# Another DMA queue for the weights, earlier weight conversion and another split of the first transpose, in a fused gated linear attention and MLP kernel

## The chip, the cores and the metric

The kernel runs on one core of a Trainium2 chip. The metric is the device time of one execution in microseconds; the time before is the median of five runs.

## The reference, cut to what matters

```python
B, H, S, D = (4, 8, 768, 48)               # attention, float32
f = 1.0 / (1.0 + np.exp(-f_logit))
for t in range(S):
    state = f[:, :, t, :, None] * state + np.einsum('bhd,bhe->bhde', k[:, :, t], v[:, :, t])
    y[:, :, t] = np.einsum('bhd,bhde->bhe', q[:, :, t], state)
x = y.transpose(0, 2, 1, 3).reshape(B * S, H * D)    # 3072 tokens x 384
h = x @ w_in                                # 384 x 2048
g = h * (1.0 / (1.0 + np.exp(-1.702 * h)))
out = g @ w_out                             # 2048 x 384
```

The inputs q, k, v, f_logit are random in float32. The MLP weights come in float64 and are made float32 on the chip.

## The kernel before, in words

The 3072 tokens are cut into 12 units of 256 tokens (4 batches of 3). A unit has an attention part and an MLP part. `attention(n)` gives a list of parts for unit n, and `merge(n, fill, ...)` plays them in order and puts MLP matmuls of earlier units, taken from the list `fill`, between them. So TensorE (PE) does the attention of unit n and the MLP of unit n-1 and before in one stream. Units 0 to 3 are emitted under an order written out by hand for all engines (`fill_order`); from there on only PE's order is by hand. Each engine takes its queue in order.

**Attention of a unit.** Raw gates f, queries q and keys k are loaded by SP (`load_raw`; L260 for the first three units, L267 after) and transposed: in units 0 to 2 by PE and ACT (L344, L349), from unit 3 on by DVE (L332). The gates of unit 3 go through a sigmoid on ACT (L337, which needs a table load before and after it among the MLP's activations). POOL multiplies gates in pairs (`begin_gates`, tile tot, L383). Then come six levels in pairs of tokens, quads and so on: ACT sets the keys of a level aside (tile Kc, L448, queries Qc L454), PE makes scores (sc, L392), DVE multiplies queries and keys by the gates in place (tile X: L473 in units 0 to 2, L477 after) and puts the scores into A (L421, L441). At the end of a unit PE computes y from A and v (L488) and the change of the state (L576), DVE updates the state st (L591, L594, L595), and PE adds the state's share to y (L616). L616 of a unit is emitted after the first promotion L477 or L473 of the next unit.

**The bridge.** y lies in PSUM. It is copied to SBUF as yT (L627), eight copies of 48 rows x 256 elements, one for each of two directions, two groups of 128 tokens and two halves of the heads. In unit 0 four of these are on ACT and four on DVE, in turn. Then `to_x` moves yT into xT, the MLP's input, with six DMAs (L649, L654): from SP's queue, but from ACT's in unit 0. PE then makes h from xT and w_in (L785), ACT the activation g (L789), PE the output o from g and w_out (L811), and ACT or DVE gather sums (L848, L850).

**The weights.** They come in 16 pairs of 128-row blocks, in order: two pairs of w_in, two of w_out, and so on. `fetch_weights` loads the 64-bit words of a pair into one of three buffers (tile bits); the first pair goes over ACT's queue, the others over SP's. A pair of w_in takes two DMAs, one of w_out one. `convert` does one step of a pair at a time: ACT's L217, then on DVE L219 and L220 (shift and mask, integer), L221 (reads bits, and so frees the buffer) and L222 (writes w_in or w_out). When a pair is through, the next fetch is asked for. How many steps go into which unit is said in the calls of `merge`: the argument `pieces` times two is the number of steps, and `by` tells in which share of the unit they should be over. Before, unit 1 takes 24 steps, unit 2 takes 20 and unit 3 takes 14.

From unit 3 on an output unit is done with seven products instead of eight (L762), for which DVE makes sums of w_out blocks (tiles T, L679) after the weights are there.

Of the kernel before, what the change touches and what calls it, by code (L numbers as in the profile page):

```python
# [16 lines left out]
def view(t, offset, dims):  # L17

    a = t[:]
    return bass.AP(a.tensor, a.offset + offset, [list(a.ap[0])] + [list(d) for d in dims])  # L20
# [3 lines left out]
def kernel(  # L24
# [33 lines left out]
    nc = tc.nc  # L58
    B, H, S, D = q.shape
    DM = H * D  # L60
# [4 lines left out]
    U = 256  # L65
# [3 lines left out]
    NP = H // 2  # L69
    HS = 64  # L70
    LEV = [1 << i for i in range(C.bit_length() - 1)]
    NL = len(LEV)
    NK = DM // P
# [60 lines left out]
    at = [wp.tile([P, n], I32, tag="bits", name=f"at{j}", bufs=PAIRS_AHEAD) for j, n in enumerate((1, NL * 64))]  # L134
# [16 lines left out]
    def query(n, f):  # L151

        return ((2, 3), (4, 5) if n < N_FILL else (0, 5))[n % 2][f]
# [16 lines left out]
    for r in range(NGR):  # L170
        ffs = range(r * FG, (r + 1) * FG)
        for ff in ffs[::2]:
            f = slice(ff * P, (ff + 2) * P)
# [9 lines left out]
    fetched, todo = {}, []  # L183
    state = {"fetch": 0, "begin": 0, "done": 0}

    def fetch_weights(engine=nc.sync):
        n = state["fetch"]
        if n >= len(pairs):
            return
        state["fetch"] += 1  # L190
        dst, parts = pairs[n]
        if moe_w_in.dtype == F32:
            for part, src in parts:
                nc.sync.dma_start(out=part(dst), in_=src)
            return
        bits = wp.tile([P, 2 * DM * 2], I32, tag="bits", name=f"bits_{n}", bufs=PAIRS_AHEAD)
        by_dst = bits.rearrange("p (c f) -> p c f", c=dst.shape[1])
        for part, src in parts:
            engine.dma_start(out=part(by_dst), in_=src.bitcast(I32))
        fetched[n] = by_dst.rearrange("p c (f two) -> p c f two", two=2)  # L200
# [25 lines left out]
    def convert():  # L226

        if state["begin"] < len(pairs) and len(todo) <= NOP // 2:
            begin_pair(state["begin"])
            state["begin"] += 1  # L230
        if todo and todo[0]:
            todo.pop(0)()
        if todo and todo[0] is None:
            todo.pop(0)
            state["done"] += 2
            fetch_weights()
# [63 lines left out]
    def rows(h):  # L300
        return slice(h * HS, h * HS + D)
# [4 lines left out]
    def attention(n):  # L306
# [10 lines left out]
        t = {"tms": [F]}  # L317
        parts = []

        def part(kind):  # L320
            return lambda fn: parts.append((kind, fn))
# [85 lines left out]
        def columns(h, g):  # L407

            return rows(h ^ g)
# [188 lines left out]
        @part("W")  # L598
        def _():

            py = t["py"]
            for cs in ((1, 0), (2, 3)):
                for a in range(NP):
                    for c in cs:
                        g, f = CHUNK[c]
                        w = HS
                        if t["before"][c] is None:
                            if not n:  # L610
                                continue
                            w = 1
                        for h in range(2):
                            state = t["before"][c][rows(h), a] if w > 1 else t["ahead"][rows(h), NC - 1, a]
                            x = a * HALF + g * HS
                            nc.tensor.matmul(  # L616
                                py[columns(h, g), g, a, f, :w], lhsT=state, rhs=X[rows(h), query(n, f), x:x + w],
                                start=False, stop=True, skip_group_check=True,
                            )
            yT = att.tile([P, NP, NG, G], F32, tag="kn", name=f"yT_{n}", bufs=1)  # L620
            xT = xTs[n] = mlp.tile([P, NK, width(n)], F32, tag="xT", name=f"xT_{n}", bufs=3)
            for f in (1, 0):
                for g in range(NG):
                    for h in range(2):
                        at, step = (g * HS, 1) if f else (U - 1 - g * HS, -1)
                        copy = nc.vector.tensor_copy if n == 0 and h else nc.scalar.copy
                        copy(view(yT[rows(h)], at, [[U, NP], [step, HS]]), py[columns(h, g), g, :, f, :])  # L627
            to_x(lambda h: (yT[rows(h), :NK], lambda r, d: yT[r:r + d, NK]), xT[:, :, :U], NG)
            if n == NALL - 1:

                pl = ps.tile([P, NP], F32, tag="mm", name="y_last", bufs=4)
                for a in range(NP):
                    for h in range(2):
                        nc.tensor.matmul(
                            pl[rows(h), a:a + 1], lhsT=last["st"][rows(h), NC - 1, a], rhs=q_end[rows(h), a:a + 1],
                            start=True, stop=True,
                        )
                yl = att.tile([P, NP], F32, tag="q_last", name="yT_last", bufs=1)
                for h in range(2):
                    nc.scalar.copy(yl[rows(h)], pl[rows(h)])  # L640
                yl = yl.rearrange("p (a g t) -> p a g t", g=1, t=1)
                to_x(lambda h: (yl[rows(h), :NK], lambda r, d: yl[r:r + d, NK]), xT[:, :, U:], 1)

        def to_x(y, x, ng):

            queue = nc.sync if n else nc.scalar
            for h in range(2):
                most, rest = y(h)
                queue.dma_start(out=x[h * D:(h + 1) * D].rearrange("p c (g t) -> p c g t", g=ng), in_=most)  # L649
                at = 0  # L650
                while at < D:
                    c, p = (h * D + at) // DR, (h * D + at) % DR
                    w = min(D - at, DR - p)
                    queue.dma_start(  # L654
                        out=x[D2 + p:D2 + p + w, c].rearrange("p (g t) -> p g t", g=ng), in_=rest(h * HS + at, w)
                    )
                    at += w
# [114 lines left out]
    def width(n):  # L772

        return U + (n == NALL - 1)
# [80 lines left out]
    def mlp_blocks(*blocks):  # L855

        hs, os = zip(*(mlp_block(n, r) for n, r in blocks))
        return sum(hs, []) + sum(os, [])
# [3 lines left out]
    LAG = 18 * DM  # L862
# [45 lines left out]
    def merge(n, fill, columns, share, pieces=0, hold=0, by=1.0, chores=(), deal=()):  # L908

        parts = parts_of(n)
        total = sum(share(kind) for kind, _ in parts)
        converting = {"W": 3, "T": 3, "B": 1} if n < N_FILL - 1 else {"W": 3, "V": 4, "S": 3, "T": 1, "B": 1}
        total_ops = sum(converting.get(kind, 0) for kind, _ in parts)
        held = sum(share(kind) for kind, _ in parts[:hold])
        at = at_ops = done = ops = 0
        for kind, fn in parts:
            ready = state["done"]
            fn()  # L920
            for chore in chores[:2]:
                chore()
            chores = chores[2:]
            at += share(kind)
            at_ops += converting.get(kind, 0)
            most = pieces * NOP // 2
            n_ops = min(int(most * at_ops / (by * total_ops)), most) - ops
            if deal:
                n_ops, deal = deal[0], deal[1:]
            ops += n_ops  # L930
            first, n_columns = done, max(0, columns * (at - held) / (total - held) - done)

            def some(end):
                nonlocal done
                while fill and done < end and fill[0][2] <= ready:
                    w, emit, _ = fill.pop(0)
                    emit()
                    done += w
            for i in range(n_ops):
                some(first + n_columns * i / n_ops)  # L940
                convert()
            some(first + n_columns)
# [8 lines left out]
    UNIT = NFF * NK * U + U // P * NFF * DM  # L951

    load_raw(0, 0)
    load_raw(0, 2)
    load_raw(0, 1, (nc.scalar,))
    fetch_weights(nc.scalar)
    begin_f, *begin = units[0][0]
    begin_f()
# [5 lines left out]
    load_raw(1, 1)  # L964
    load_raw(1, 2)
    fetch_weights()
    fetch_weights()
    fill = []
# [1 line left out]
    fill += mlp_blocks((0, 0)) + mlp_blocks((0, 1))  # L970
    merge(1, fill, UNIT // 2 - LAG // 2 - 3 * DM, steady, 12, hold=2)
    fill += mlp_blocks((1, 0), (1, 1)) + mlp_blocks((0, 2), (1, 2))
    merge(2, fill, UNIT + 3 * DM, steady, 10)
    fill += mlp_blocks((2, 0), (2, 1)) + mlp_blocks((2, 2), (0, 3)) + mlp_blocks((1, 3), (2, 3))
    merge(3, fill, 3 * UNIT // 2 - LAG // 2, steady, 7, by=0.7)
    fill_order.close()
    for n in range(3, NALL):
        fill += mlp_unit(n)
# [36 lines left out]
```

## Time and profile before

| | |
|---|---|
| median of five runs | 630.69 us (627.81 to 631.24) |
| the profiled execution | 629.54 us, its span 627.8 us |
| PE busy | 605.2 us (96%) |
| DVE busy | 385.9 us (61%) |
| ACT busy | 260.5 us (41%) |
| POOL busy | 39.9 us (6%) |
| granted TensorE clock, mean | 0.984 |
| DMA | 58.21 MB, nearly all on the queue of SP |

Busy time is the time in which an engine has an instruction running; a wait of PE is a gap. "PE h L785" is PE's instruction from line 785 that writes tile h. Tiles are named without their number. An arrow points from what is read to what is written (`out<-in`), or from a waiting instruction to what released it. All times in the stage tables are us from the start of the span.

### The profile page before, as it was taken

To read this page: it belongs to the slowest core of one execution; us is meant where nothing else is said; L and a number is where in the kernel's file an instruction comes from. 1 tells how busy PE (TensorE), PEld (TensorE's weight loads), DVE (VectorE), ACT (ScalarE), POOL (GpSimd) and SP (SyncE) were. 2 spreads that over 40 slices of the span, in tenths; PEclk is the share of its full clock that TensorE was granted. 3 is DMA by queue.
4 is the path that set the end of the run, shared out by engine and by line. 5 is a ranking of instruction groups with operands and counts; after the bars stand their busy time and mean duration, and the time that the engine had idled before them with its cause. 6 is when DMAs were issued, how large, how long until landed. Compare 5 with 4: busy or idle time off the path is not lost.

```text
span 627.8 us, 17094 instructions
## 1 busy us (share of the span) xinstructions
PE 605.2 (96%) x7314; PEld 519.2 (83%) x7314; DVE 385.9 (61%) x632; ACT 260.5 (41%) x544; POOL 39.9 (6%) x91
## 2 busy tenths in 40 slices
PE   7969999889999999999999999999999999999997
PEld 5647776757678688989989989989989889889896
DVE  1879976475876755677566577656658645521441
ACT  3536542533344534543544454354354353233220
POOL 3010110020001001001001001001001001000000
PEclk9968999889999999999999999999999999999999
DMA  6656766642034434444452342542161121001000
GB/s 173 181 154 151 176 148 171 153 114 76 2 92 99 123 102 103 105 97 106 122 135 60 76 108 73 142 122 68 45 160 33 44 59 27 27 1 27 26 1 25
DMA packets 83309, 58.21 MB, mean 93 GB/s; under 512 B 33634, under 2 KB 75266, under 8 KB 83234
## 3 DMA queue, kind: packets, MB, share of 16 engines
q1 hardware_dynamic: 82192, 55.55, 35.1%
q10 hardware_dynamic: 1041, 1.57, 1.0%
q8 instruction: 57, 0.93, 0.6%
q14 instruction: 19, 0.15, 0.1%
HBM read 43.98 MB, written 8.39 MB: 83 GB/s over the span
## 4 chain that ended last, share of the span: by engine, by line
PE 87%; DVE 7%; ACT 3%; DMA 1%; issue 1%; SPq 1%; ACTq 0%; DVEq 0%
PE h L785 38%; PE o_X L762 8%; PE o_Y L762 8%; PE o L811 8%; PE o_Z L762 7%; PE sc L392 6%; PE o_W L762 4%; PE t L344 2%; PE y L616 2%; PE sc L576 2%; PE y L488 1%; ACT yT L627 1%; DVE X L473 1%; DVE a L221 1%; PE idle L108 1%
## 5 line engine op out<-in xcount | busy, mean ns | idle before, releaser
L785 PE MATMUL h<-xT,w_in 128*128 128x256 f32 (+1 forms) x1152 | 259.5, 383 | 2.4 <-ACT g L789 1.9
L785 PEld LDWEIGHTS h<-xT,w_in 128*128 128x128 f32 x1152 | 218.0, 191 | 34.9 <-ACT g L789 2.1
L789 ACT ACTIVATE g<-h 128x256 f32<-128x256 f32 (+1 forms) x192 | 72.2, 384 | 157.8 <-PE h L785 157.6
L477 DVE TENSOR_TENSOR X<-X,tot 128x1024 f32<-128x1024 f32 x45 | 55.1, 1223 | 62.7 <-PE sc L392 49.4
L448 ACT COPY Kc<-X 128x512 f32<-128x512 f32 x72 | 48.0, 666 | 81.4 <-DVE X L477 51.4
L811 PE MATMUL o<-w_out,g 128*128 128x384 f32 x192 | 67.5, 501 | 3.0 <-DVE w_out L222 3.0
L811 PEld LDWEIGHTS o<-w_out,g 128*128 128x128 f32 x192 | 36.3, 194 | 25.9 <-DVE w_out L222 3.6
L762 PE MATMUL o_X<-w_out,g 128*128 128x192 f32 x288 | 52.6, 331 | 0.0
L762 PE MATMUL o_Y<-T,S 128*128 128x192 f32 x288 | 51.9, 329 | 0.0
L441 DVE COPY_PREDICATED A<-masks,sc 128x256 f32<-128x256 uint32 (+1 forms) x108 | 50.9, 535 | 0.1
L762 PEld LDWEIGHTS o_Y<-T,S 128*128 128x128 f32 x288 | 46.9, 190 | 1.5 <-issue 0.7
L762 PEld LDWEIGHTS o_X<-w_out,g 128*128 128x128 f32 x288 | 46.7, 190 | 1.0
L383 POOL TENSOR_TENSOR tot<-F 128x512 f32<-128x512 f32 x12 | 12.5, 1040 | 478.1 <-DVE st L594 428.7
L332 DVE STREAM_TRANSPOSE X<-raw 128x512 f32<-128x512 f32 x36 | 37.9, 1101 | 2.9 <-PE y L616 2.8
L392 PEld LDWEIGHTS sc<-X,Kc 48*64 48x64 f32 x1440 | 26.4, 138 | 14.8 <-ACT Kc L448 8.5
L392 PE MATMUL sc<-X,Kc 48*64 48x64 f32 x1440 | 31.1, 224 | 7.5 <-ACT Kc L448 6.3
L700 DVE TENSOR_TENSOR g<-g,g 128x512 f32<-128x512 f32 x18 | 12.5, 692 | 40.4 <-ACT g L789 40.4
L627 ACT COPY yT<-y 48x256 f32<-48x256 f32 x92 | 33.8, 367 | 8.5 <-PE y L616 6.0
L473 DVE TENSOR_TENSOR X<-X,tot 128x512 f32<-128x512 f32 x30 | 20.4, 690 | 11.2 <-PE sc L392 10.3
L762 PE MATMUL o_W<-T,g 128*128 128x192 f32 x144 | 24.9, 326 | 0.0
L762 PE MATMUL o_Z<-T,g 128*128 128x192 f32 x144 | 24.9, 326 | 0.0
L762 PE MATMUL o_Z<-w_out,g 128*128 128x192 f32 x144 | 24.9, 326 | 0.0
(92 smaller groups left out, 629.2 us busy)
## 6 DMA issues: line engine op xcount, KB each, us to landing
bits<-in_moe_w_out_dram SPq DMA_DIRECT2D x8, 768.0 KB, 5.3
raw<-in_f_logit_dram SPq DMA_DIRECT2D x48, 96.0 KB, 2.3
raw<-in_k_dram SPq DMA_DIRECT2D x48, 96.0 KB, 2.3
raw<-in_q_dram SPq DMA_DIRECT2D x44, 96.0 KB, 2.4
bits<-in_moe_w_in_dram SPq DMA_DIRECT2D x7, 576.0 KB, 5.9
k_tok<-z SPq DMA_DIRECT2D x56, 64.0 KB, 1.7
kt<-k_tok SPq DMA_DIRECT2D x14, 256.0 KB, 2.9
out_dram<-osb SPq DMA_DIRECT2D x18, 192.0 KB, 1.8
```

The source lines that it names most:

```text
L332: nc.vector.transpose(view(out, at, [[HALF, NP], [step, R4], [R4 * step, 32]]), by_half[:, j, f].rearrange("p a (j d) -> p (a j) d", j=R4) ...
L344: nc.tensor.matmul(pt[h * HS:(h + 1) * HS, jj, :], lhsT=by_pair[j][:, h, x:x + HS], rhs=ident, start=True, stop=True)
L392: nc.tensor.matmul(t["sc"][g * HS:(g + 1) * HS, h, a, s, :], lhsT=t["Kc", l][rows(h), x:x + HS], rhs=rhs(h, a, g), start=True, stop=True,)
L441: nc.vector.copy_predicated(out=view(A, at, dims), mask=mask.bitcast(U32), data=got)
L448: nc.scalar.copy(c.rearrange("p (n two m) -> p n two m", two=2, m=m), view(X, KF * SLOT, [[2 * m, SLOT // (2 * m)], [(KR - KF) * SLOT + m, ...
L473: nc.vector.tensor_tensor(x, x, y, ALU.mult)
L477: nc.vector.tensor_tensor(x, x, y, ALU.mult)
L627: copy(view(yT[rows(h)], at, [[U, NP], [step, HS]]), py[columns(h, g), g, :, f, :])
L762: nc.tensor.matmul(t[bank], lhsT=lhs(f), rhs=rhs(f), start=(new and f == 0), stop=(f == HF - 1), skip_group_check=True,)
L785: nc.tensor.matmul(ph, lhsT=w_in[:, c, ff * P:(ff + 1) * P], rhs=xTs[n][:, c, :], start=(c == 0), stop=(c == NK - 1))
L789: nc.scalar.activation(g[ff // FG][:, ff % FG, :], ph, AF.Gelu_apprx_sigmoid)
L811: nc.tensor.matmul(t["po"], lhsT=g[ff // FG][:, ff % FG, tt * P:(tt + 1) * P], rhs=w_out[:, ff, :], start=(ff == ffs[0]), stop=(ff == ffs[ ...
```

## The change

Three things change. `fetch_weights` issues its DMAs from GpSimd's (POOL's) queue instead of SP's; only the first pair stays on ACT's queue. The steps of conversion are dealt out otherwise: unit 2 gets 34 steps (17 x 2), due in 0.9 of the unit, and unit 3 gets none. In unit 0 each of the eight yT copies is cut by pairs of heads: ACT copies the first three pairs (48 rows x 192) and DVE the fourth (48 rows x 64); and the six xT DMAs of unit 0 are issued by SP, as those of all other units are.

```diff
-    def fetch_weights(engine=nc.sync):
+    def fetch_weights(engine=nc.gpsimd):
...
                         at, step = (g * HS, 1) if f else (U - 1 - g * HS, -1)
-                        copy = nc.vector.tensor_copy if n == 0 and h else nc.scalar.copy
-                        copy(view(yT[rows(h)], at, [[U, NP], [step, HS]]), py[columns(h, g), g, :, f, :])
+                        most = NK if n == 0 else NP
+                        nc.scalar.copy(
+                            view(yT[rows(h)], at, [[U, most], [step, HS]]), py[columns(h, g), g, :most, f, :]
+                        )
+                        if n == 0:
+                            nc.vector.tensor_copy(
+                                view(yT[rows(h)], NK * U + at, [[step, HS]]), py[columns(h, g), g, NK, f, :]
+                            )
...
-            queue = nc.sync if n else nc.scalar
             for h in range(2):
                 most, rest = y(h)
-                queue.dma_start(out=x[h * D:(h + 1) * D].rearrange("p c (g t) -> p c g t", g=ng), in_=most)
+                nc.sync.dma_start(out=x[h * D:(h + 1) * D].rearrange("p c (g t) -> p c g t", g=ng), in_=most)
...
-                    queue.dma_start(
+                    nc.sync.dma_start(
...
-    merge(2, fill, UNIT + 3 * DM, steady, 10)
+    merge(2, fill, UNIT + 3 * DM, steady, 17, by=0.9)
...
-    merge(3, fill, 3 * UNIT // 2 - LAG // 2, steady, 7, by=0.7)
+    merge(3, fill, 3 * UNIT // 2 - LAG // 2, steady)
```

## The prediction

> **What bounds the kernel now.** I read the page's first two parts, then busy time by stage, then who waited for whom, then the order of time on ACT and DVE at two places. Columns of the stage rows: start and end, length, busy time (instructions) of PE, its weight loads, DVE, ACT, POOL, then TensorE's granted clock, DMA share and GB/s.
>
> ```profile
> PE 605.2 (96%) x7314; PEld 519.2 (83%) x7314; DVE 385.9 (61%) x632; ACT 260.5 (41%) x544; POOL 39.9 (6%) x91
> ```
> ```profile
> 40.00:60.00 20.00, 15.47 (x185) 12.00 (x185) 17.32 (x30) 10.62 (x20) 0.40 (x2) 0.73 0.58 143
> 60.00:80.00 20.00, 19.26 (x373) 14.52 (x370) 19.11 (x32) 12.04 (x27) 3.09 (x5) 1.00 0.75 171
> 80.00:100.00 20.00, 19.83 (x168) 14.77 (x167) 14.73 (x26) 7.46 (x16) 1.65 (x2) 1.00 0.61 141
> 100.00:120.00 20.00, 18.14 (x129) 12.56 (x128) 12.91 (x20) 9.19 (x14) 0.00 (x0) 0.98 0.68 178
> 120.00:140.00 20.00, 16.87 (x293) 12.02 (x292) 10.51 (x17) 5.71 (x12) 4.19 (x6) 0.85 0.57 138
> ...
> 160.00:180.00 20.00, 20.00 (x139) 14.97 (x139) 17.64 (x24) 5.51 (x12) 0.00 (x0) 1.00 0.13 33
> ```
>
> From 146 us on PE hardly rests (from 300 to 628 us it is busy for 324 of 328). What the change is worth is therefore decided before 146 us, in three places: 37 to 56, where PE waits; 56 to 79, where DVE is full (19.11 of 20) and PE follows it; 116 to 146, where PE waits again. The matmul order of both kernels is the same, row for row.
>
> ```profile
> PE sc L392 <- ACT Kc L448: 6.3, 4, 3.7
> PE o L811 <- DVE w_out L222: 3.0, 1, 3.0
> ...
> PE h L785 <- ACT g L789: 1.9, 1, 1.9
> ...
> PE h L785 <- DMA xT<-yT: 0.5, 1, 0.5
> ```
>
> Those are the waits at 41.6 (3.7 us), 129.1 (3.0), 116.7 (1.9) and 145.5 us. The first, in order of time on ACT, and the third place, on DVE:
>
> ```profile
> 37.47 0.37 ACT L627 COPY yT<-y 48x256 f32<-48x256 f32 x1 [1.37 <-PE y L616]
> 38.33 0.37 ACT L627 COPY yT<-y 48x256 f32<-48x256 f32 x1 [0.49 <-DVE yT L627]
> ...
> 40.44 0.60 ACTq L649 DMA_DIRECT2D xT<-yT  x1
> ...
> 43.34 1.24 ACTq L654 DMA_DIRECT2D xT<-yT  x2
> 44.62 0.67 ACT L448 COPY Kc<-X 128x512 f32<-128x512 f32 x1 [4.21 <-DVE a L221]
> ```
> ```profile
> 126.43 0.35 DVE L595 TENSOR_TENSOR st<-st,sc 128x192 f32<-128x192 f32 x1 [6.28 <-PE sc L576]
> ...
> 129.04 1.72 DVE L221 SCALAR_TENSOR_TENSOR a<-bits,a 128x768 f32<-128x768 uint32 x1
> 130.80 1.25 DVE L222 TENSOR_TENSOR w_out<-a,s 128x768 f32<-128x768 f32 x1
> ...
> 132.64 2.01 DVE L332 STREAM_TRANSPOSE X<-raw 128x512 f32<-128x512 f32 x2
> 136.17 1.23 DVE L477 TENSOR_TENSOR X<-X,F 128x1024 f32<-128x1024 f32 x1 [1.52 <-ACT Qc L454]
> ```
>
> The reader is to see that Kc sits behind six issues on ACT's own queue, and that two engines take yT in strict turns; then that after the last w_out wait (132.1) the same DVE queue still has k's transposes and L477 before y's matmuls, which start at 137.46.
>
> [...]clock 0.50 from 37.3 to 50.9, from 119.2 to 122.6 and from 132.9 to 136.2 us[...].[...] L221, 0.96 us elsewhere, takes 1.72 beside POOL's tot at 128.9.
>
> **Part 1, the first yT and xT.** Now four rounds of ACT 0.37 and DVE 0.42 with 0.03 us between: 0.855 each, 3.42 in all. After: eight rounds of 48x192 on ACT and 48x64 on DVE, and in the built order every one still waits for the one before it on the other engine. ACT: 0.315 (48x256 takes 0.37, 128x192 0.31). DVE: 0.225, an estimate from 0.355 at 192 and 0.42 at 256 elements and 0.19 for a 64-element row. With 0.06 between, 0.60 a round, 4.8 in all: DVE is free **1.38 us later**, at 42.27. What ACT gains: its six issues (40.44 to 44.58) are gone, so Kc starts 0.73 after L473, at 43.0 instead of 44.62, and PE at 43.7 instead of 45.34. But DVE sets the rest of this unit. Its three waits there go: L473 at 45.39 for Kc (0.82 beyond the start-to-start step), at 46.54 (0.54) and 52.70 (0.76) for scores. 2.12 minus 1.38: **0.74 earlier** from 52.7 on, and so through 79 us. On SP the six xT issues, 3.6 us from 41.4, stand ahead of the loads of q and k for unit 2; these are needed at 58 and 72 us, so they cost nothing. xT lands by about 48 to 49; its matmuls can't start before 48.
>
> **Part 2, the queue of the weights.** 22 issues leave SP and stand on POOL between the groups of tot. Each waits for the L221 that frees its buffer, and tot waits behind it: tot of unit 2 (76.6 us) stands behind pair 9, freed at 71.5; tot of unit 3 (128.9) behind pair 15, freed at 105. Nothing waits. Data: pair 7 is freed at 62.6 and needed by ACT at 71 us; it landed 6.3 us after its issue[...]. In unit 2 each pair has 9 us or more.[...] Below: nothing. Above: two of them held for a length each, 1.1 us, for each of some five pairs on the path, 5.6 us. I take **1.0**.
>
> **Part 3, conversions into unit 2.** From L473 at 76.7 to F's transposes at 111.2 DVE now has 13 conversion rows; after, 26. Four rows are 3.06 us start to start, so 10 us more. Its idle time there is 9.3 (1.30, 2.09, 1.71, 1.33, 2.49, 0.36), of which 1.2 stays, before the last scores. So F's transposes start at 111.2 - 0.74 + 10 - 8.1 = 112.4; laid out row by row I get 112.65, ending 114.55. ACT: sigmoid 1.06, then a table load 1.28, but no L217 (0.89) between them any more: g at 116.95 instead of 118.12, matmuls at 117.4, **1.16 earlier** (this holds the 0.74). The idle time is then 1.45 instead of 1.87; I keep the half clock. L595 starts at 125.27.
>
> Behind it w_out no longer keeps PE: the 3.0 go, and **y's matmuls take the wait over**. Between the last st and k's transposes DVE has L220, L221, L222 of pair 15 and a sum, beside tot: 1.3 + 1.25 + 1.15 + 0.46 = 4.2 instead of 3.5; after the transposes two T rows (1.74) fill the 1.52 that ACT needs. L477 comes 0.7 later against L595. PE is out of work at L595 + 5.9 and gets y at L595 + 11.7: 5.8 us idle, so y and the scores after it run at half clock (32 score matmuls: 1.13 instead of 0.69 us at 37.6). y takes 1.8 instead of 1.1, which delays yT and xT by 0.7; scores and 18 o's then make PE itself 0.8 later than xT. Sum at 146 us: -1.16 + 0.7 + 0.7 + 0.8 = +1.04. The relief of DVE after 146 (7 conversion groups, T) buys nothing: PE is full there.
>
> **Sum.** +1.04 + 1.0 = +2.0 against the profiled execution, 629.54 (span 627.8): 631.6. The median shown, 630.69, is 1.15 above it: **632.7**, 0.3% slower, and 0.3% (1.9 us) is about what a measurement of this kernel can tell from no change.
>
> **Rivals.**
> 1. Not slower: the shorter wait for g (1.45) keeps full clock. For it: 0.81 us at 54 and 1.63 at 14.5 did not lower the clock; against: 1.87 did. Then the 1.9 us lost in 18 matmuls (5.84 instead of 3.9) return until DVE binds, its row before L595 ending at 124.0: L595 2.4 earlier, the sum -0.2, and 629.3, or 630.5 by the median. If y too escapes, 1.5 less, 629.0.[...] Chance 0.26.
> 2. [...]its queue in units 1 and 2 is nearly full, so every hold counts: +5.6 instead of 1.0, some 637. For it: L473 2.47 instead of 1.29 beside tot[...]. 0.22.
> 3. Weights come late: if POOL's fetch takes 9 us instead of 6, pair 7 is 1 to 2 us late where DVE is full: 634 to 635. 0.10.
> 4. yT isn't shared at all but taken in turns: that is in my forecast.
>
> **Numbers.** The likeliest case has 0.42, its own range 631 to 634.5, half on each side of 632.6. Range 628.8 to 637. Faster: half of rival 1, 0.12. Same: 0.14 of it and 0.20 of the likeliest, 0.34. Slower: 0.22, 0.22 and 0.10, 0.54.
>
> **What would show it.** yT ends near 42.3 and Kc starts near 43; the wait on w_out at L811 is gone; a wait of PE on L477 of 4 us or more ahead of y; F's transposes end near 114.5; half clock after that wait. I am wrong if h of unit 2 starts before 145 us, if the sixteen yT copies overlap, or if L219 and L220 stay at 0.56 while the time still rises.

## The result and the profile after

| | before | after |
|---|---|---|
| median | 629.65 us (626.88 to 632.42, 79 runs) | 630.84 us (629.2 to 633.98, 44 runs) |
| ratio, 95% interval | | 1.0025 (1.0015 to 1.0034) |
| profiled execution, its span | 629.54, 627.8 us | 631.68, 629.9 us |
| POOL busy | 39.9 us | 54.5 us |

So the change makes the kernel 0.25% slower (0.15% to 0.34%), about the 0.3% that the prediction took as the least that can be told from no change. First the page's busy time and the stage table of the kernel after, with the columns explained in the prediction:

```profile
PE 603.9 (96%) x7314; PEld 519.5 (82%) x7314; DVE 386.5 (61%) x636; ACT 261.3 (41%) x548; POOL 54.5 (9%) x113
```
```profile
40.00:60.00 20.00, 14.64 (x178) 11.64 (x178) 17.44 (x34) 11.73 (x24) 4.77 (x10) 0.83 0.75 156
60.00:80.00 20.00, 19.22 (x378) 14.36 (x375) 19.03 (x32) 11.84 (x26) 5.78 (x8) 1.00 0.61 163
80.00:100.00 20.00, 19.45 (x167) 14.49 (x166) 18.47 (x31) 9.28 (x19) 6.04 (x10) 1.00 0.80 197
100.00:120.00 20.00, 18.00 (x128) 12.11 (x127) 18.84 (x28) 8.43 (x12) 1.46 (x2) 1.00 0.87 201
120.00:140.00 20.00, 13.70 (x226) 10.54 (x230) 18.19 (x26) 6.26 (x13) 4.18 (x6) 0.91 0.42 97
```

DVE is now nearly as full from 80 to 140 us (18.5, 18.8 and 18.2 of 20) as it was before from 60 to 80 alone (19.11). At 80 to 100 the DMA share rose from 0.61 to 0.80. From 120 to 140 PE lost another 3.2 us (16.87 to 13.70). The waits of PE from 30 to 150 us in the kernel after (total us, times, longest):

```profile
PE y L616 <- DVE X L477: 5.6, 1, 5.6
PE sc L392 <- DVE A L421: 4.5, 1, 4.5
PE h L790 <- ACT g L794: 2.7, 1, 2.7
...
PE h L790 <- DMA xT<-yT: 0.4, 1, 0.4
```

The wait on w_out is gone and y waits 5.6 us for L477 in its place. Two waits are new in kind: the first scores of unit 1 wait for A (L421), not Kc, and h waits for xT at 88.6 us. In order of time, DVE in the first unit, then ACT at F, then DVE behind the last state rows, all of the kernel after:

```profile
43.44 0.22 DVE L631 COPY yT<-y 48x64 f32<-48x64 f32 x1 [0.38 <-ACT yT L627]
43.69 1.29 DVE L473 TENSOR_TENSOR X<-X,F 128x512 f32<-128x512 f32 x2
44.90 0.68 DVE L421 TENSOR_TENSOR A<-sc,masks 128x512 f32<-128x512 f32 x1
```
```profile
116.64 1.28 ACT L337 ACT_TABLE_LOAD   x1 [1.68 <-DVE F L332]
117.93 1.06 ACT L337 ACTIVATE F<-F 128x1024 f32<-128x1024 f32 x1
119.00 1.28 ACT L794 ACT_TABLE_LOAD   x1
120.30 0.38 ACT L794 ACTIVATE g<-h 128x256 f32<-128x256 f32 x1
```
```profile
126.92 0.35 DVE L595 TENSOR_TENSOR st<-st,sc 128x192 f32<-128x192 f32 x1 [1.50 <-PE sc L576]
...
129.53 1.32 DVE L220 TENSOR_SCALAR a<-s 128x768 int32<-128x768 int32 x1
130.89 1.25 DVE L221 SCALAR_TENSOR_TENSOR a<-bits,a 128x768 f32<-128x768 uint32 x1
132.18 1.04 DVE L222 TENSOR_TENSOR w_out<-a,s 128x768 f32<-128x768 f32 x1
133.14 0.54 DVE L855 TENSOR_TENSOR sum<-sum,o 128x384 f32<-128x384 f32 x1
133.60 1.99 DVE L332 STREAM_TRANSPOSE X<-raw 128x512 f32<-128x512 f32 x2
135.45 0.93 DVE L684 TENSOR_TENSOR T<-w_out,T 128x768 f32<-128x768 f32 x1
136.31 0.93 DVE L684 TENSOR_TENSOR T<-w_out 128x768 f32<-128x768 f32 x1
137.17 1.20 DVE L477 TENSOR_TENSOR X<-X,F 128x1024 f32<-128x1024 f32 x1
```

The last sixteen-turn copy is followed at once by L473 and L421, for which PE waits. The first table load starts only when F's transposes are over (116.5 us), so two loads and a sigmoid, 3.7 us, lie between F and g. And pair 15's conversion, a sum, k's transposes and two T rows stand between the state and L477, as the prediction laid them out.

**A clock for comparing traces.** The first yT starts at 37.47 us before and at 38.88 after. The traces put that down to a stretch of half clock near 17 us (granted clock 0.50 from 17.5 to 20.5 us), which e3 has too and which isn't the change's doing (see e4). All runs are therefore compared from the first yT on. All times in this table are us after it; "level 3" is the third level's L441 of unit 1, F the first transpose of F of unit 3 (111.22 us from the span's start before), h the matmuls that waited for g (118.56), st the first of unit 2's last L595 rows (126.43), and h2 the start of h of unit 2 (146.03). The runs marked e and f are the experiments.

| | median, us | ratio, 95% interval | level 3 | F | h | st | h2 |
|---|---|---|---|---|---|---|---|
| before | | | 15.84 | 73.75 | 81.09 | 88.96 | 108.56 |
| after | 630.84 | 1.0025 (1.0015, 1.0034) | 15.07 | 75.65 | 81.85 | 88.04 | 109.71 |
| e1, queue alone | 630.50 | 1.0020 (1.0007, 1.0034) | 15.69 | 75.63 | 82.98 | 89.16 | 108.77 |
| e2, dealing alone | 643.00 | 1.0221 (1.0202, 1.0240) | 16.55 | 85.00 | 91.21 | 99.69 | 121.47 |
| e3, first part alone | 628.02 | 0.9994 (0.9978, 1.0010) | 15.07 | 72.95 | 80.28 | 88.16 | 107.81 |
| e4, after, pairs 1, 2 on SP | 632.77 | 1.0053 (1.0032, 1.0074) | 15.08 | 75.92 | 82.14 | 88.32 | 109.97 |
| e6, xT on SP alone | 626.88 | 0.9968 (0.9955, 0.9981) | 13.68 | 71.55 | 78.89 | 85.08 | 104.70 |
| e7, e6 and yT side by side | 625.80 | 0.9957 (0.9936, 0.9979) | 12.35 | 70.22 | 77.56 | 83.75 | 103.38 |
| e8, queue and dealing | 633.48 | 1.0083 (1.0061, 1.0106) | 15.34 | 77.56 | 83.79 | 91.66 | 113.19 |
| e9, e7, queue, 11 and 6 pieces | 624.34 | 0.9937 (0.9915, 0.9958) | 12.34 | 71.31 | 77.53 | 83.71 | 102.53 |
| f1, e1 with pair 10 on SP | 629.23 | 0.9991 (0.9978, 1.0003) | 15.87 | 73.79 | 81.13 | 89.00 | 108.75 |
| f3, after, yT side by side | 630.98 | 1.0026 (1.0007, 1.0045) | 14.02 | 75.29 | 81.51 | 89.38 | 110.88 |
| f4, e9 with pair 10 on SP | 624.90 | 0.9939 (0.9916, 0.9961) | 12.33 | 71.23 | 77.44 | 83.63 | 102.45 |
| f5, f3 with pairs 4, 10 on SP | 627.73 | 0.9990 (0.9974, 1.0006) | 12.34 | 72.24 | 78.45 | 84.64 | 106.27 |

Ratios are to runs of the kernel before on the same chip. What follows h2 takes 481.77 us before and 481.31 after.

### The profile page after: what moved, and what is told of

Same layout as the page of the kernel before. It is cut to its first block, busy times and chain, and to the rows that moved or that the text cites. A ratio compares the mean times of both kernels' runs of the same rounds, so it can differ in the third digit from the quotient of the medians.

```text
span 629.9 us, 17112 instructions
## 1 busy us (share of the span) xinstructions
PE 603.9 (96%) x7314; PEld 519.5 (82%) x7314; DVE 386.5 (61%) x636; ACT 261.3 (41%) x548; POOL 54.5 (9%) x113
## 4 chain that ended last, share of the span: by engine, by line
PE 82%; DVE 8%; DMA 5%; ACT 2%; issue 2%; SPq 1%; DVEq 0%
PE h L790 36%; PE o_X L767 8%; PE o_Y L767 8%; PE o_Z L767 7%; PE o L816 6%; PE sc L392 5%; PE o_W L767 4%; DMA raw<-in_q_dram 2%; PE y L616 2%; PE t L344 2%; PE sc L576 2%; PE y L488 1%; DMA raw<-in_k_dram 1%; DVE a L221 1%; DVE X L473 1%
## 5 line engine op out<-in xcount | busy, mean ns | idle before, releaser
L477 DVE TENSOR_TENSOR X<-X,tot 128x1024 f32<-128x1024 f32 x45 | 55.1, 1224 | 67.2 <-PE sc L392 55.8
L816 PE MATMUL o<-w_out,g 128*128 128x384 f32 x192 | 66.2, 494 | 0.0
L441 DVE COPY_PREDICATED A<-masks,sc 128x256 f32<-128x256 uint32 (+1 forms) x108 | 51.0, 535 | 0.1
L627 ACT COPY yT<-y 48x256 f32<-48x256 f32 (+1 forms) x96 | 34.8, 362 | 9.1 <-PE y L616 6.0
L383 POOL TENSOR_TENSOR tot<-tot 128x256 f32<-128x256 f32 (+4 forms) x60 | 24.6, 410 | 4.7
```

Source lines behind the costliest of these rows:

```text
L383: nc.gpsimd.tensor_tensor(tn, t2[:, :, 0], t2[:, :, 1], ALU.mult)
L441: nc.vector.copy_predicated(out=view(A, at, dims), mask=mask.bitcast(U32), data=got)
L477: nc.vector.tensor_tensor(x, x, y, ALU.mult)
L627: nc.scalar.copy(view(yT[rows(h)], at, [[U, most], [step, HS]]), py[columns(h, g), g, :most, f, :])
L816: nc.tensor.matmul(t["po"], lhsT=g[ff // FG][:, ff % FG, tt * P:(tt + 1) * P], rhs=w_out[:, ff, :], start=(ff == ffs[0]), stop=(ff == ffs[ ...
```

## The experiments

**e1, the queue alone.**

```diff
-    def fetch_weights(engine=nc.sync):
+    def fetch_weights(engine=nc.gpsimd):
```

> The kernel before, with the weights' DMAs on GpSimd's queue and nothing else changed. Theory (the queue costs by order: the fetch of pairs 1 and 2 goes ahead of the raw q and k of unit 1, pair 10 ahead of xT of unit 1): first tot of unit 0 near 9.3 us, then L219 and the first yT about 1.4 us later than before, a wait of PE on xT of unit 1 near 88 us, another 0.6 us; L219 and L220 stay at 0.56 us. The end +1.0 to +2.1 us against before. Rival A (the queue costs nothing, the added time comes from the conversions and the yT copies): within 0.4 us of before. Rival B[...]: L219 and L220 longer than 0.6 us, +2 us or more.

The end is +0.20%, as the theory said, but half of its reason falls: the first yT starts at 36.79 us, earlier than before, although pairs 1 and 2 went out early here too. The other half holds. Waits of PE from 80 to 95 us in e1, then its fetch on POOL:

```profile
PE h L785 <- DMA xT<-yT: 1.4, 2, 1.0
```
```profile
80.93 0.75 POOL L199 DMA_DIRECT2D bits<-in_moe_w_out_dram  x1
```

The six xT issues of unit 1 stand on SP from 78.7 to 82.5; pair 10 goes out in their middle, where the kernel before issued it at 83.32, behind them. F is 1.88 late. In this trace 1.7 of it comes back at st, because the 18 matmuls of h ran at full clock: 6.18 us from h to st instead of 7.87, at a granted clock of 1.00 from 112 to 127 us instead of 0.89. The groups of L219 and L220, in e1:

```profile
L219 DVE TENSOR_SCALAR s<-a 128x768 int32<-128x768 int32 x16 | 8.9, 559 | 3.6 <-ACT a L217 2.8
L220 DVE TENSOR_SCALAR a<-s 128x768 int32<-128x768 int32 x16 | 8.9, 555 | 0.3
```

559 and 555 ns each, against 561 and 556 before: GpSimd's fetches didn't lengthen these rows. Rival B is out.

**f1, e1 with pair 10 back on SP.**

```diff
         dst, parts = pairs[n]
+        engine = nc.sync if n == 10 else engine
```

> The kernel before, weights on GpSimd's queue, but pair 10 alone on SP's, where it stands behind xT of unit 1 as before. Theory (pair 10, issued on GpSimd in the middle of xT's six issues, delays xT of unit 1: 1.4 us of PE waits in the kernel with the queue alone): no wait of PE on xT near 86 to 88 us above 0.3, F's transposes 73.7 to 74.3 us after the first yT (75.63 with the queue alone, 73.75 before), L219 and L220 still at 0.56 us; the end -0.5 to +0.6 us against before. Rival (another DMA or GpSimd's own time delays xT): the waits stay and F's transposes are still at 75 us or later, the end +1.3 us.

No wait on xT is left from 80 to 112 us, F is at 73.79 (75.63 with the queue alone, 73.75 before), and the end is level with before. So the queue's whole cost at F is one fetch that overtakes xT of unit 1.

**e2, the dealing alone.**

```diff
-    merge(2, fill, UNIT + 3 * DM, steady, 10)
+    merge(2, fill, UNIT + 3 * DM, steady, 17, by=0.9)
-    merge(3, fill, 3 * UNIT // 2 - LAG // 2, steady, 7, by=0.7)
+    merge(3, fill, 3 * UNIT // 2 - LAG // 2, steady)
```

> The kernel before, with all conversions through by the end of unit 2 (17 pieces due in 0.9 of it, none in unit 3) and nothing else changed. Theory: F's transposes start about 1.2 to 2 us later than the 111.2 before, and the table load with them, so h's matmuls after g start at 119.5 to 120.5 instead of 118.56; the wait of o on w_out is gone; PE waits over 5 us for L477 ahead of y at half clock; h of unit 2 starts 1 to 1.5 us later than 146.0 if the 18 matmuls of h run at full clock, 2.5 to 3 us later if they run at half clock. The end +1.0 to +3.0 us. Rival (the dealing of the conversions costs nothing, all of the added time is the late loads): within 0.4 us of before.

Neither came true: +2.2%, 13 to 14 us. DVE, then SP's queue in e2:

```profile
109.46 0.56 DVE L219 TENSOR_SCALAR s<-a 128x768 int32<-128x768 int32 x1 [9.48 <-ACT a L217]
```
```profile
84.71 0.53 SPq L199 DMA_DIRECT2D bits<-in_moe_w_out_dram  x1
...
103.94 0.39 SPq L199 DMA_DIRECT2D bits<-in_moe_w_out_dram  x1
```

Between two fetches of weights SP issues the raw f, q and k of unit 3, for 19 us. Conversions that are asked for earlier find no weights: DVE idles 9.48 us and F starts 11.25 later. On the old queue, in this order of issues, the dealing can't work; the new queue costs little by itself (e1) and is what makes the dealing possible (e8). The parts don't add up, which neither of my cases had.

**e8, queue and dealing, without the first part** (the edits of e1 and e2 together).

> The kernel before, with the weights on GpSimd's queue and the conversions dealt as in the change: the change without its first part. Theory (the dealing alone cost 13 us because pairs 11 and on were fetched behind the 24 raw loads of unit 3 on SP; on a queue of their own they are not): h of unit 2 about 110.5 us after the first yT (108.56 before), the end +1 to +2.8 us, no idle time of DVE for L217 near 100 us. Rival (the dealing costs 10 us whatever the queue and the first part hides it): +8 us or more.

The idle time near 100 us is gone and the 13 us with it, so the reason is confirmed; my number isn't: +0.83%, and h2 at 113.19. Of the 3.48 us between e8 and the change at h2, 0.27 lie at level 3, 1.64 between there and F (xT of unit 1 is waited for 1.5 us instead of 0.43) and 1.68 between h and st, which is the half clock on the 18 matmuls: 7.87 us there in e8, 6.19 in the change, after a wait of PE for g of nearly the same length (2.8 and 2.7 us). On the new queue the dealing thus adds 0.63% (0.83 against e1's 0.20), and the first part, which alone brings 0.06% (e3, within its noise), takes 0.58% of it back.

**e3, the first part alone** (the diff of yT and xT, nothing else).

> The kernel before, with only the first unit's yT cut by pairs of heads and its xT on SP's queue. Theory: sixteen copies in turns end 1.4 us later on DVE, Kc starts near 43, L441 of the third level of unit 1 ends 0.7 to 0.8 us earlier than before, and this stays through 108 us: the end -0.2 to -0.9 us. Rival (the turns cost more than the freed ACT queue gives): L441 of the third level later than before, the end +0.3 to +1.4 us.

Level 3 is 0.77 earlier, and this is kept: 0.80 at F, 0.75 at h2. The median's interval (-0.22% to +0.10%) holds the expected size and zero. The instructions up to the first yT are those of the kernel before, and yet it starts at 38.91 us, as in the change (see e4).

**e4, the change with pairs 1 and 2 on SP.**

```diff
-    fetch_weights()
-    fetch_weights()
+    fetch_weights(nc.sync)
+    fetch_weights(nc.sync)
     fill = []
```

> The changed kernel, with pairs 1 and 2 alone fetched from SP's queue again, behind the raw loads of unit 1. Theory (these 1.5 MB, issued at 12.5 us, hold up the raw q and k): the first yT is back at 37.5 us, 1.4 us earlier than in the changed kernel; h of unit 2 and the end 0.7 to 1.4 us earlier than in the changed kernel, so about -0.2 to +0.7 us against before. Rival (the early 1.4 us come from elsewhere, GpSimd's own time or the lower clock at 17 us): the first yT stays at 38.5 us or later, the end within 0.3 us of the changed kernel, +1.2 us against before.

The first yT moved (37.89), but the theory falls all the same: the end did not come earlier (+0.53% against +0.25%, intervals that overlap). What makes the first yT late in the change (38.88) and in e3 (38.91) stands in the traces. These are the two executions that show a granted clock of 0.88 from 14 to 28 us; the others show 1.00. The first three groups of score matmuls of unit 0, before (two of them), then after:

```profile
16.09 0.70 PE L392 MATMUL sc<-X,Kc 48*64 48x64 f32 x32 [1.63 <-ACT Kc L448]
...
21.11 0.69 PE L392 MATMUL sc<-X,Kc 48*64 48x64 f32 x32 [0.62 <-DVE A L441]
```
```profile
16.12 0.70 PE L392 MATMUL sc<-X,Kc 48*64 48x64 f32 x32 [1.63 <-ACT Kc L448]
...
19.30 1.13 PE L392 MATMUL sc<-X,Kc 48*64 48x64 f32 x32
...
22.54 0.69 PE L392 MATMUL sc<-X,Kc 48*64 48x64 f32 x32 [0.56 <-DVE A L441]
```

They start together, so no load had landed late; the second group then takes 1.13 us instead of 0.70, and the third starts 6.42 us after the first instead of 5.02. The clock granted in the change from 17.5 to 20.5 us is 0.50. In e3 the distance is 6.19, in the other twelve executions 5.01 or 5.02. So the change's 1.4 us is a stretch of half clock, and e3 has one as well, without the new queue.

In the other executions the first yT goes with the queue, and the other way than I expected: it lies between 36.09 us (f5) and 37.06 (f1) in the seven executions with pairs 1 and 2 on POOL, and between 37.23 (e6) and 38.04 (e2) in the five with them on SP, this run among these. On average POOL's is 0.9 us earlier. What brings this was not tested, and a comparison from the first yT on leaves it out.

**e6, xT of unit 0 on SP and nothing else.**

```diff
-            queue = nc.sync if n else nc.scalar
+            queue = nc.sync
```

> The kernel before, with the six xT DMAs of unit 0 on SP's queue and nothing else changed: yT stays in four rounds of turns. Theory (the freed ACT queue pays 2.1 us, the cut by pairs costs 1.4 of them): L441 of the third level of unit 1 starts about 13.7 to 14.4 us after the first yT, against 15.84 in the kernel before and 15.07 with both edits; h of unit 2 about 107.0 us after the first yT (108.56 before), the end -1.2 to -2.1 us. Rival (the cut by pairs is what pays, or the score wait on L421 keeps the gain): 15 us or more, the end within 0.5 us of before.

Level 3 at 13.68, 2.16 earlier than before and 1.39 earlier than with the cut by pairs; the end -0.32%. That is the prediction's sum of part 1 taken apart: 2.12 gained from ACT's queue, 1.38 given back by the sixteen turns. At h2 this trace is 3.86 earlier than before; 1.68 of that is the clock on the matmuls of h (6.19 us from h to st instead of 7.87), which no run ties to the edit.

**e7, e6 with yT side by side.** Each engine copies half of the heads into its own SBUF tile, and y has one PSUM tile for each group of tokens; the two engines take the groups in opposite order.

```diff
+            yTs = [yT, att.tile([P, NP, NG, G], F32, tag="yT2", name="yT2", bufs=1) if n == 0 else yT]
...
+                        g = i ^ h if n == 0 else i
...
-                        copy(view(yT[rows(h)], at, [[U, NP], [step, HS]]), py[columns(h, g), g, :, f, :])
+                        copy(view(yTs[h][rows(h)], at, [[U, NP], [step, HS]]), py[g][columns(h, g), :, f, :])
```

> The kernel before, with xT of unit 0 on SP's queue, and the first yT written into two tiles and read from two PSUM tiles, so that ACT and DVE copy side by side instead of in turns. Theory (turns cost DVE 3.4 us before and 4.8 in the change, side by side it is some 1.8): L473 starts about 1.8 us after the first yT, L441 of the third level 12.0 to 13.2 us after it, and the end -2.2 to -3.8 us. Rival (another wait takes it over: scores at half clock, Kc, or a raw load or pair 7 at 58 to 72 us): no earlier than the kernel with xT on SP alone.

DVE in e7, then ACT:

```profile
37.42 1.78 DVE L629 COPY yT<-y 48x256 f32<-48x256 f32 x4
39.24 1.40 DVE L473 TENSOR_TENSOR X<-X,F 128x512 f32<-128x512 f32 x2
```
```profile
37.36 1.79 ACT L629 COPY yT<-y 48x256 f32<-48x256 f32 x4 [1.27 <-PE y L616]
```

Four copies on each engine over the same 1.8 us, without a wait. L473 starts 1.88 after the first yT, level 3 at 12.35, another 1.33 earlier, kept to h2. The end is -0.43%; against e6 the intervals overlap, so the last step is shown by the trace alone. Which of the two, the SBUF tiles or the PSUM tiles, ends the turns was not tried apart.

**f3, the change with yT side by side** (the edit of e7 on the change).

> The whole change, but the first yT copied side by side by ACT and DVE, half of the heads each, into two tiles from two PSUM tiles, instead of in sixteen turns. Theory (turns: 4.8 us of DVE's time in the change, 1.9 side by side, worth 1.4 + 1.2 us as between the three kernels with only this part): L473 1.9 us after the first yT, h of unit 2 about 106.5 to 107.5 us after it (109.71 in the change), the end 2 to 3 us earlier than the change, -0.5 to -1.5 us against before. Rival (the gain is lost at xT of unit 1 or the late F path): within 0.7 us of the change, +0.9 to +1.6 us against before.

The rival is right: +0.26%, level with the change. Waits of PE from 40 to 60 us in f3, then POOL's fetch:

```profile
PE h L787 <- DMA xT<-yT: 3.2, 2, 2.6
```
```profile
42.47 1.28 POOL L199 DMA_DIRECT2D bits<-in_moe_w_in_dram  x2 [1.77 <-DVE a L221]
```

In f3 xT of unit 0 is issued from 38.85 to 43.43, and pair 4 goes out on POOL before the last of it; in e7 it stands on SP at 45.07, behind.

**f5, f3 with pairs 4 and 10 on SP.**

```diff
+        engine = nc.sync if n in (4, 10) else engine
```

> The whole change with yT side by side, as in f3, but pairs 4 and 10 on SP's queue, behind the xT issues of units 0 and 1. Theory (those two fetches, issued on GpSimd in the middle of xT's issues, caused PE's waits on xT of 2.6, 0.7 and 0.5 us and so ate the gain of f3): these waits gone or under 0.3 us, L441 of the third level of unit 1 about 12.4 us after the first yT (14.02 in f3), F's transposes at 72.5 to 73.8 (75.29), the end 1.5 to 2.5 us earlier than f3, about 0 to -1.5 us against before. Rival (DVE, full with conversions, or the wait on L477 holds it anyway): F's transposes at 75 us and the end within 0.5 us of f3.

Level 3 at 12.34, F at 72.24, waits on xT 0.2 in all, and -0.10% instead of +0.26% in f3 (the intervals don't overlap). It is the f1 finding a second time: with these fetches behind xT, what the side-by-side copy brings is kept through the change. y still waits 5.6 us for L477.

**e9, a version against both.** e7, the weights on POOL, and 11 pieces in unit 2 and 6 in unit 3, so that no conversion row stands between the state and k's transposes.

```diff
+    merge(2, fill, UNIT + 3 * DM, steady, 11, by=0.8)
+    merge(3, fill, 3 * UNIT // 2 - LAG // 2, steady, 6, by=0.75)
```

> A version meant to beat both: yT side by side and xT on SP as in e7, weights on GpSimd's queue, and conversions dealt 11 pieces into unit 2, due in 0.8 of it, 6 into unit 3, due in 0.75. So pair 11 is through before F's transposes and no conversion stands between the last st L595 and k's transposes. Theory: no wait of PE on w_out, L477 about 5 us after L595 starts its last row instead of 9.7, the wait of PE ahead of y under 1.5 us and y at full clock; the end 3 to 6 us earlier than before. Rival (what is cleared is taken over by the next wait: xT of unit 2, ACT's Kc and Qc, or F's path at half clock): within 1 us of e7.

-0.63%, 624.34 us: faster than both kernels. The wait on w_out is gone; the one ahead of y is 3.4, not 1.5. DVE in e9:

```profile
122.97 0.35 DVE L595 TENSOR_TENSOR st<-st,sc 128x192 f32<-128x192 f32 x1
124.66 0.55 DVE L852 TENSOR_TENSOR sum<-sum,o 128x384 f32<-128x384 f32 x1 [1.34 <-PE o L813]
125.14 2.02 DVE L332 STREAM_TRANSPOSE X<-raw 128x512 f32<-128x512 f32 x2
128.67 1.23 DVE L477 TENSOR_TENSOR X<-X,F 128x1024 f32<-128x1024 f32 x1 [1.51 <-ACT Qc L454]
```

With the conversion gone, DVE waits 1.34 us for PE's o in a sum ahead of the transposes, and 1.51 for ACT ahead of L477: 8.05 us from L595 to L477 instead of 9.74. Against e7 h2 is 0.85 earlier; the medians' intervals overlap, so that the new queue and dealing gain anything over e7 isn't shown.

**f4, e9 with pair 10 on SP.**

> The version with the conversions dealt 11 and 6 and yT side by side, with pair 10 on SP's queue. Theory (that version had no wait on xT of unit 1, so there is little to win): within 0.7 us of it, -3.4 to -5 us against before. Rival (the queue still costs it a part of the 1.3 us): a further 0.8 to 1.3 us earlier.

-0.61%, level with e9, which had no wait on xT there.

## Why the prediction was right, and where it was not

The forecast was 0.3% slower and the result is 0.25% slower, well inside the range. The three places were right, and so were most steps between them; that the number fits so closely is in part luck, as the end of this section says. Step by step, again in us after the first yT (the prediction's times less 37.47):

| | before | predicted | after |
|---|---|---|---|
| last yT ends on DVE | 3.39 | 4.80 | 4.78 |
| Kc starts | 7.15 | 5.53 | 5.53 |
| F | 73.75 | 75.18 | 75.65 |
| h after g | 81.09 | 79.93 | 81.85 |
| st | 88.96 | 87.80 | 88.04 |
| L477 | 98.70 | 98.24 | 98.29 |
| h2 | 108.56 | 109.60, 110.60 with the contention | 109.71 |

- **Part 1 holds**, in both its terms (e3, e6): 0.74 predicted, 0.77 measured. One step in it was off: PE was to start its scores at 43.7 us, 6.2 after the first yT; they started 6.85 after it, because they wait for L421, which stands on DVE behind the turns. It costs nothing at level 3.
- **The contention of 1.0 us measured nothing.** It was my estimate of how long L219 and L220 would be held beside GpSimd's fetches, and no trace had shown such a hold. In the change ten of the 32 rows run beside a fetch instruction, and each took 0.56 us (the one L220 of 1.32 us, at 129.53, runs beside POOL's tot). What the queue does cost was not in the working: "nothing waits" looked at the weights being late, and not at what they overtake. xT of unit 1 is late by 1.4 us of PE's waits with the queue alone, 0.43 in the change. Rivals 2 and 3 are out: no fetch lengthened L219 or L220, and no conversion waits for a pair in the change. No run puts pair 10 back into the change as it stands; f5 does so, with pair 4, beside the side-by-side copy.
- **F** came 0.47 later than laid out row by row, which is about the size of that wait on xT (0.43); that the wait is the cause is shown for the queue alone (f1), not for the change.
- **h after g was off by 1.92**, of which 0.47 is F. Of the other 1.45, the table load is 1.28: I had it over before F was ready, but it starts after F's last transpose, so it comes in series. The last 0.17 stays open.
- **The half clock was the other way.** In this execution the 18 matmuls kept full clock after a wait of 2.7 us (granted clock 1.00 from 112 to 127 us, 0.89 before), which gave 1.68 back (6.19 instead of 7.87 from h to st). Rival 1 tied the clock to the wait's length; that step is wrong, as the last section shows. That this error and the one before it cancel to 0.24 at st is luck.
- **Behind st** the prediction has L477 0.7 later against L595 (measured 10.25 instead of 9.74, 0.51), y at half clock 1.8 us (1.96), and 2.2 us in all from st to h2; measured 2.07 (21.67 instead of 19.60).

Of the signs that I named against myself the last came true: L219 and L220 stayed at 0.56 while the time rose. The rise lies in the other terms: from the first yT on, the trace has +1.15 at h2 and -0.46 behind it, 0.69 us in all, where parts 1 and 3 of the forecast had 1.04 and the contention 1.0 more. The medians differ by 1.2 us, and by about 1.6 (0.25%) against runs on the same chips; what lies between these and the 0.69 no single pair of traces can tell.

So the direction and the waits were foreseen, and the size was lucky in three ways. Without the 1.0 for a contention that isn't there the forecast would have been +1.04, or 0.17%. The late g and the full clock cancel. And the profiled execution took the 631.68 us that I had forecast (631.6) only because the 1.41 us of half clock ahead of its first yT, which isn't the change's, fills the gap.

## What to carry to other kernels

One DMA queue for small urgent and large patient transfers is an order, and taking the large ones to another queue removes it: look for what they will overtake (here xT, at two places: PE waited 1.4 us for it in e1 and 3.2 in f3), and leave those few where they were. Two engines that are to share a copy may take turns instead: here they ran side by side once each had tiles of its own in SBUF and in PSUM (1.8 us in e7), and until then the number of turns set the time, not the bytes (the same bytes took 3.39 us in eight turns and 4.78 in sixteen). And parts of a change are not to be priced one by one when one of them (the queue) supplies what another (the earlier conversion) consumes.

## What the runs showed of the hardware that I had not expected

- **The length of a wait didn't tell the clock after it.** After the same wait of PE for g, 1.9 us, h's matmuls ran at half clock in the kernel before, e3 and f1 (7.87 or 7.88 us from h to st, granted clock 0.89 from 112 to 127 us) and at full clock in e1, e6 and e7 (6.18 or 6.19, granted clock 1.00). After 2.7 to 2.8 us they ran at full clock in the change, e4 and f5 (1.00), and at half clock in e8 and f3 (0.89). The y matmuls of e9 still ran at full clock after 3.4 us (1.11 us in all), and at half clock in the change after 5.6 (1.96). What decides it no run shows.
- **One kernel scatters by its clock.** Of the 35 runs of the kernel before beside e1 to e4, the 15 with a mean granted clock of 0.992 took 628.5 us on average and the 7 with 0.984 to 0.986 took 631.0. A single profile carries that 2.5 us, more than the whole effect sought here. What the mean counts can be worked out: the three stretches at 0.50 that the prediction lists for the profiled execution before last 20.3 us, and half of that is 0.016 of its 627.8 us, just what its mean of 0.984 lacks. By this estimate a step of 0.0027 in the mean is one stretch of 3.4 us, as long as the one from 119.2 to 122.6 us, which is 1.7 us of full clock lost. Of the 133 runs of the kernel before beside all experiments 53 have a mean of 0.992 or more, of the change's 44 none. At equal clock the change is 0.9 us slower at 0.989 (629.9 against 629.0, means) and 1.2 at 0.986 (632.1 against 631.0), so the rest of the 2.0 us between the means of all runs (631.1 and 629.2) goes with the lower clock.
- **GpSimd's fetches were cheap for the others.** Its instruction takes 0.63 us for w_in and 0.74 for w_out. Its data land after 6.0 and 6.5 us in the change, against 5.9 and 5.3 from SP before; but e1, which moves the queue alone, has 6.1 and 5.3, so no longer transfer is shown. L219 and L220 kept their length, 0.56 us, while beside POOL's tot one L220 took 1.32.
- **The table load waited with the activation that it serves.** The load of 1.28 us ahead of F's sigmoid began at 116.64 us, after F's last transpose, although ACT had been idle for 1.68 us. In e4, e8, f3 and f5 it was the same after 1.69 to 1.71 us of idle ACT, in e9 and f4 after 0.7.
